# A WaveNet convolution block: the first loads in halves on two queues, fewer warm-up products, one extra tap moved, and the last gate on GpSimd

## The chip, the cores and the metric

The kernel runs on one core of a Trainium2 chip. A core has TensorE (PE in the profile, for matrix products, with PEld for the load of the fixed operand), VectorE (DVE), ScalarE (ACT), GpSimd (POOL), SyncE (SP, which issues transfers) and 16 DMA engines that all queues share. The metric is the device time of one execution in microseconds (us), and lower is better. Times are compared as medians of several runs.

## The reference

`x` is a batch of 2 sequences of 16000 time steps with 256 channels, in bfloat16. A causal convolution with three taps and dilation 2 gives 512 channels. The first 256 go through tanh, the others through a sigmoid, their product is projected by a 256x256 matrix.

```python
dil, K = 2, 3
pad = (K - 1) * dil                      # 4 rows of zeros ahead
xp = jnp.pad(x, ((0, 0), (pad, 0), (0, 0)))
h = sum(einsum('btc,cd->btd', xp[:, pad - i*dil : pad - i*dil + T], w[i]) for i in range(K))
z = jnp.tanh(h[..., :D]) * sigmoid(h[..., D:])
out = z @ w_o
```

So tap `w[0]` meets the step itself, `w[1]` the step two back and `w[2]` the step four back.

## The kernel before, in words

**Groups and blocks.** Time is cut into groups. The first group is *plain*: 512 steps of sequence 0, done with the three taps as they stand. Fifteen *wide* groups of 2048 steps follow; they use a fast scheme in which sums and differences of `x` (tiles `q`, `qp`, `qm`, `qd`, made on VectorE and GpSimd) meet combined weights (`wmh`, `wph`, `wm`, `wt`, `wu`, `wd0`, `wd2`), so that fewer products are needed. Two small plain groups fill what is left: `extra` (512 steps, tiles `e_ps`, input `xte`) is mixed into the first wide blocks, and `end` (256 steps, input `xe`, tiles `th`, `sg`, `z`) is done at the end. Each group has four blocks of 128 output channels, in the order tanh, sigmoid, tanh, sigmoid (`O_ORDER`). The order of all instructions is written out by hand, and the order in the program is the order on each engine.

**The head.** `xn` (named `osb` in the profile) is the plain input with time on the partitions. SP's queue issues `xn`, then the tap `w[0]`, and then the transposing loads `xq` of the first wide group (L119), `xte` (L105) and `xq` of the second. ScalarE's queue issues taps `w[2]` and `w[1]` (`TAPS` is (2, 0, 1), the order in which the plain blocks use them) and then loads its activation table (L135). TensorE meanwhile does 14 products of a tile of zeros, 256 columns each (L140). Then `turn` transposes `xn` on TensorE in eight 128x128 pieces (L184), ScalarE and VectorE copy the results into `xt` (L186), and 40 products of the four plain blocks follow (L311, function `direct`). VectorE and ScalarE form the combined weights as the taps arrive (L421 to L426); two of them are made on TensorE by `weight_mm` (L172). The first wide blocks begin with `first` (L255), which reads `qp`.

**A wide block** in the steady loop runs on TensorE: `late(V, 0)` for the block before it (L247, weights `wt` and `wu`), `second` (weights `wph`, input `qm`), the projection of finished gates (L366), `first` of the next block, `third` (weights `wm`, input `qm`), and `late(V, 1)` (weights `wd2`, `wd0`). Between them stand `keep_second` on ScalarE (L281, tile `sv`), which `third` waits for, `split_bank` on VectorE (L287), which reads what `third` wrote and which `late(V, 0)` of the next iteration waits for, `other` on GpSimd (L284) and `rest` on VectorE (L291). Index `ND` (4) is the first wide block. `extra_block(i, taps)` does block `i` of the extra group for the taps given; its activation follows the last tap.

**The tail.** After the last wide block the four remaining projections of the group before (`left`, in two pairs), eight of the last group (`last_pieces`), and the end group are finished. `plain_ends` does the end group's convolution for tanh or sigmoid (L311) and its activation on ScalarE (L587); `gate(end, ...)` is its product on VectorE (L342), written so that four time phases interleave; its projection is one `out_mm` with its copy at L649 and its store at L650. `gate_phases` gates half of the last group (L593). `last_pieces` copies one projected piece on ScalarE and one on VectorE (both L615) and stores them (L624, or each on a queue of its own, L617). Tiles named `o_ps` have two buffers, so a projection that uses one waits until the copy two projections back is done.

Of the kernel before, what the change touches and what calls it, by code (L numbers as in the profile page):

```python
# [8 lines left out]
ACT = mybir.ActivationFunctionType  # L9
# [4 lines left out]
def kernel(  # L14
# [23 lines left out]
    nc = tc.nc  # L38
# [4 lines left out]
    P = 128  # L43
# [8 lines left out]
    TAPS = (2, 0, 1)  # L52
# [4 lines left out]
    for b in range(B):  # L57
        t, stop = (4 * 2 * P if b == 0 else 0), (T - 4 * RE if b == B - 1 else T)
        while t < stop:
            n = min(need, (stop - t) // 8)  # L60
# [8 lines left out]
    end = dict(wide=False, b=B - 1, r0=T // 4 - RE, R=RE, g="z")  # L69
# [18 lines left out]
    def new_y():  # L88
        return ps_y.tile([P, 2, BANK], f32, name="y")
# [38 lines left out]
    w_taps = [consts.tile([P, CT, D2], bf16, name=f"w{k}_sb") for k in range(K)]  # L128
    wo_sb = consts.tile([P, NT, D], bf16)
    xn = osb_pool.tile([P, 4, D], bf16, name="osb")  # L130
    w_in = [w[k].rearrange("(ct c) d -> c ct d", c=P) for k in range(K)]
    nc.sync.dma_start(out=xn[:], in_=x[0, 0:4 * P, :].rearrange("(r j) c -> r j c", j=4))
    for k in (TAPS[0], TAPS[2]):
        nc.scalar.dma_start(out=w_taps[k][:], in_=w_in[k])
    nc.scalar.preload_act_table(ACT.Sigmoid)  # L135
    nc.sync.dma_start(out=w_taps[TAPS[1]][:], in_=w_in[TAPS[1]])
    for n in range(14):
        if n < 6 and n % 2 == 0:
            wps = new_y()
        nc.tensor.matmul(  # L140
            wps[:, 1, (n % 2) * 256:(n % 2 + 1) * 256], lhsT=warm[:, :P], rhs=warm[:, :256],
            start=n % 2 == 0 and n < 6, stop=True, skip_group_check=True,
        )
# [149 lines left out]
    def direct(B, taps, out, new=True, h0=None):  # L293

        xt, R = B.G["x"], B.R
        if B.G is not end:
            xp, yp, xc, yc = views(B.G)
        for tap in taps:
            if B.G is end:
                parts = [(None, xt[:, 4 - 2 * tap:8 - 2 * tap])]  # L300
            elif tap == 1:
                parts = [(0, yp), (1, xc)]
            elif h0 is not None:
                parts = [(h0, (xp, yp)[h0])]
            else:
                lo = RH if tap == 0 else RH - 1
                parts = [(None, xt[:, :, :, lo:lo + R])]
            for h, mv in parts:
                to = out if h is None else out[:, 2 * h * R:2 * (h + 1) * R]
                for ct in range(CT):  # L310
                    nc.tensor.matmul(  # L311
                        to, lhsT=w_taps[tap][:, ct, B.osl], rhs=mv[:, :, ct, :],
                        start=new and tap == TAPS[0] and ct == 0 and not h, stop=tap == TAPS[-1] and ct == CT - 1,
                        skip_group_check=True,
                    )
# [9 lines left out]
    def activate(B, src):  # L325
        G = B.G
        act_tiles(G)
        o = B.o
        func = ACT.Tanh if o < NT else ACT.Sigmoid
        dst = G["th"][:, o] if o < NT else G["sg"][:, o - NT]  # L330
        if src == "sv":
            nc.scalar.activation(out=dst[:, 2:4, :], in_=B.sv[:], func=func, scale=0.25)  # L332
        elif src == "y":
            nc.scalar.activation(out=dst[:, 0:2, :], in_=B.y[:], func=func, scale=0.25)  # L334
        else:
            nc.scalar.activation(out=dst, in_=src.rearrange("p (j r) -> p j r", j=4), func=func, scale=1.0)

    def gate(G, dts, eng=nc.vector):
        z = G["z"][:, dts]
        if G is end:  # L340
            z = z.rearrange("p t r j -> p t j r")
        return eng.tensor_tensor(out=z, in0=G["th"][:, dts], in1=G["sg"][:, dts], op=ALU.mult)  # L342
# [60 lines left out]
    ND = 4  # L403
# [39 lines left out]
    def extra_block(i, taps):  # L443
        E = extras[i]
        if TAPS[0] in taps:
            E.y = ps_o.tile([P, BANK], f32, name="e_ps", tag="o_ps")
        direct(E, taps, E.y[:])
        if TAPS[-1] in taps:
            activate(E, E.y[:])
# [11 lines left out]
    def do(steps, k):  # L461
        ins = None
        for step in steps.pop(k, []):
            ins = step() or ins
        return ins
# [36 lines left out]
    for k in range(ND, NB):  # L502
        B, V = blocks[k], (blocks[k - 1] if k > ND else None)

        E = {ND: (0, TAPS[2:]), ND + 1: (1, TAPS[2:]), ND + 2: (2, TAPS), ND + 3: (3, TAPS)}.get(k)
        if k == ND + 1:
            extra_block(1, TAPS[:2])
        if V:
            late(V, 0)
        if k >= ND + 2:  # L510
            Y = blocks[k - 2]
            activate(Y, "y")
            note_gates(Y, k)
        last = do(small, k) or last

        big_late = k == ND + 1

        def big_and_quarter(last):
            last = do(big, k) or last
            if B.oi == 0 and k > ND:  # L520
                quarter(B.G, 3, last)
            elif B.oi and B.G["n"] + 1 < len(wides):
                quarter(wides[B.G["n"] + 1], B.oi - 1, last)
            return last

        if not big_late:
            last = big_and_quarter(last)
        second(B)
        keep_second(B)
        other(B, last)  # L530
        if V:
            rest(V)
        if E:
            extra_block(*E)
        if k == ND + 3:
            gates_of(extra, slice(0, 2))

        project(0 if k < ND + 3 else 1 if k < ND + 7 else 2)
        evict()
        N = blocks[k + 1] if ND < k < NB - 1 else None  # L540

        split_first = k in (ND + 2, ND + 3) or k >= ND + 7
        if N:
            first(N, 0)
            if not split_first:
                first(N, 1)
        third(B)
        split_bank(B)
        if big_late:
            last = big_and_quarter(last)  # L550
        if V:
            activate(V, "sv")
        if N:
            if split_first:
                first(N, 1)
            keep_first(N)
        if V:
            late(V, 1)
        todo += ready
        ready.clear()  # L560
        if B.oi == 0:
            if loaded_wide < len(wides):
                load_wide(loaded_wide)
                loaded_wide += 1
            elif "x" not in end:
                load_end()
# [14 lines left out]
    def plain_ends(func, i):  # L581

        for h in range(NT):
            B = ends[2 * h + i]
            direct(B, TAPS, ye[:, i, h * 4 * RE:(h + 1) * 4 * RE], h == 0)
        dst = end["sg" if i else "th"]
        nc.scalar.activation(  # L587
            out=dst[:].rearrange("p h j r -> p (h j r)"), in_=ye[:, i, :NT * 4 * RE], func=func, scale=1.0)
# [3 lines left out]
    def gate_phases(ps):  # L592
        nc.vector.tensor_tensor(out=G["z"][:, dt, ps], in0=G["th"][:, dt, ps], in1=G["sg"][:, dt, ps], op=ALU.mult)  # L593
# [11 lines left out]
    left = [todo[i:i + 2] for i in range(0, len(todo), 2)]  # L605
# [3 lines left out]
    def last_pieces(rb0, jps, where, queues=None):  # L609
        two_pieces([(G, rb0, jp) for jp in jps], where)  # L610
        osb = osb_pool.tile([P, 2, 2, D], bf16, name="osb")
        rows = out[b, t0 + 8 * rb0:t0 + 8 * (rb0 + P), :].rearrange("(p j) d -> p j d", j=8)
        at = [rows[:, 2 * jp:2 * jp + 2, :] for jp in jps]
        for i, (jp, copy) in enumerate(zip(jps, (nc.scalar.copy, nc.vector.tensor_copy))):
            copy(out=osb[:, i], in_=G["o", rb0, jp])  # L615
            if queues:
                queues[i].dma_start(out=at[i], in_=osb[:, i])  # L617
        if not queues:

            dims = [list(d) for d in at[0].ap]  # L620
            both = bass.AP(
                tensor=at[0].tensor, offset=at[0].offset,
                ap=[dims[0], [2 * (jps[1] - jps[0]) * D, 2], [1, 2 * D]])
            nc.sync.dma_start(out=both, in_=osb[:].rearrange("p i q d -> p i (q d)"))  # L624

    def left_pieces(ps, where, between=None):
        two_pieces(ps, where)
        if between:
            between()
        for i, piece in enumerate(ps):  # L630
            out_evict(*piece, i == 1)

# [5 lines left out]
    left_pieces(left[0], "o")  # L638
    last_pieces(0, (1, 2), "y")
    gate_phases(slice(0, 2))  # L640
    last_pieces(P, (1, 2), "o")
    plain_ends(ACT.Sigmoid, 1)
    left_pieces(left[1], "yy", lambda: gate(end, slice(0, 2)))
    last_pieces(0, (0, 3), "o")
    (piece,) = pieces(end)
    out_mm(*piece, y_bank(new_y(), 0))
# [2 lines left out]
    nc.scalar.copy(out=osb[:], in_=end["o", 0, None])  # L649
    nc.sync.dma_start(  # L650
        out=out[end["b"], te:te + 4 * RE, :].rearrange("(q p) d -> p q d", q=2), in_=osb[:])
    last_pieces(P, (0, 3), "o", (nc.scalar, nc.sync))


# [28 lines left out]
```

## Time and profile before

| | us |
|---|---|
| time, median of 3 runs | 265.46 (265.1 to 265.76) |
| the profiled execution's own time | 265.18 |
| its span, first to last instruction | 263.4 |
| TensorE busy | 257.0 (98%) |
| ScalarE busy | 246.5 (94%) |
| VectorE busy | 226.6 (86%) |
| GpSimd busy | 111.2 (42%) |

A row of the timeline gives the start and the duration in us, the engine, the line of the kernel, the operation, the tile written and the tiles read, the size and the count; rows of one kind that follow each other are merged. In square brackets stands how long the engine had been idle, and what ended that. A "q" behind an engine's name is its queue of transfers. Records of matrix products overlap, since they are pipelined: one of 256 columns lasts 0.27 us, but the next starts 0.11 us after it.

### The profile page before, as it was taken

The page shows a single profiled execution, that of the slowest core. Times are in us where ns is not written, and L with a number is a line of the kernel's source. Part 1 is how long each engine was busy: PE and PEld are TensorE (multiplying, and loading weights), DVE is VectorE, ACT ScalarE, POOL GpSimd, SP SyncE. Part 2 cuts the span into 40 slices and gives each one's busy share as a digit, 9 for nine tenths or more (in the row PEclk, how much of TensorE's full clock was granted, in tenths as well). Part 3 has the DMA queues.
Part 4 walks back from the last instruction along what each step waited for, and adds up shares of the span by engine and source line. Part 5 has one row for each costly group of instructions (what it writes and reads, how often), then busy time and mean ns, then how long its engine had stood idle before and what let it go on. Part 6 is the DMA issues. An engine that isn't in the chain of part 4 may idle for free.

```text
span 263.4 us, 4233 instructions
## 1 busy us (share of the span) xinstructions
PE 257.0 (98%) x1469; PEld 144.0 (55%) x1470; DVE 226.6 (86%) x262; ACT 246.5 (94%) x377; POOL 111.2 (42%) x128
## 2 busy tenths in 40 slices
PE   7999999999999999999999999999999999999993
PEld 6544544555555555555555555555555555555682
DVE  3779899898898998899889889889889988976574
ACT  3858899999999999999999999999999999999972
POOL 1025345535534544544553553454454354353200
PEclk9999999999999999999999999999999999999999
DMA  7997092472928339192762819357292834221235
GB/s 204 221 149 160 0 206 78 105 193 79 212 80 176 116 110 218 55 238 80 111 181 99 231 42 197 133 94 197 82 213 76 186 126 101 80 80 42 82 119 179
DMA packets 78789, 35.10 MB, mean 133 GB/s; under 512 B 69168, under 2 KB 70960, under 8 KB 78768
## 3 DMA queue, kind: packets, MB, share of 16 engines
q1 hardware_dynamic: 77808, 34.05, 51.8%
q10 hardware_dynamic: 960, 0.79, 1.1%
q8 instruction: 11, 0.18, 0.3%
q14 instruction: 10, 0.08, 0.1%
HBM read 1.18 MB, written 16.38 MB: 67 GB/s over the span
## 4 chain that ended last, share of the span: by engine, by line
PE 92%; DVE 5%; issue 1%; ACT 1%; DVEq 0%
PE y L247 56%; PE o_ps L366 19%; PE y L255 9%; PE y L311 3%; DVE sv L291 1%; PE e_ps L311 1%; PE y L140 1%; PE y L172 1%; DVE y L287 1%; PE y L366 1%; DVE qp L220 1%; DVE osb L615 1%; DVE q L214 0%; DVE zw L342 0%; DVE z L342 0%
## 5 line engine op out<-in xcount | busy, mean ns | idle before, releaser
L284 POOL TENSOR_TENSOR sv<-sv,st 128x512 f32<-128x512 f32 x60 | 76.4, 1273 | 25.1 <-ACT sv L281 24.7
L232 POOL TENSOR_TENSOR qd<-xq 128x256 bf16<-128x256 bf16 (+2 forms) x60 | 35.4, 592 | 110.7 <-DVE zw L342 54.0
L291 DVE TENSOR_TENSOR sv<-sv,y 128x1024 f32<-128x1024 f32 x60 | 72.7, 1212 | 3.8 <-PE y L247 3.7
L247 PE MATMUL y<-qd,wd_sb 128*128 128x512 bf16 x240 | 61.6, 379 | 0.4 <-DVE sv L291 0.3
L395 ACT CAST osb<-o_ps 128x512 bf16<-128x512 f32 x113 | 60.6, 591 | 0.2 <-PE o_ps L366 0.2
L366 PE MATMUL o_ps<-wo_sb,zw 128*128 128x256 bf16 x464 | 60.3, 273 | 0.1
L287 DVE SCALAR_TENSOR_TENSOR y<-st,y 128x512 f32<-128x512 f32 x60 | 41.8, 696 | 20.6 <-PE y L247 20.4
L366 PEld LDWEIGHTS <-zw 128*128 128x128 bf16 x480 | 47.0, 98 | 17.4 <-issue 0.2
L255 PE MATMUL y<-qp,wmh_sb 128*128 128x512 bf16 x120 | 44.3, 379 | 0.0
L247 PEld LDWEIGHTS <-wd_sb 128*128 128x128 bf16 x240 | 23.4, 98 | 29.1 <-issue 1.5
L281 ACT ACTIVATE sv<-y 128x512 f32<-128x512 f32 x60 | 35.8, 597 | 2.9 <-PE y L247 2.7
L214 DVE TENSOR_TENSOR q<-xq 128x2048 bf16<-128x2048 bf16 (+2 forms) x32 | 36.8, 1155 | 1.3 <-DMA xq<-in_x_dram 1.3
L277 ACT ACTIVATE st<-y 128x512 f32<-128x512 f32 x60 | 36.3, 607 | 0.0
L247 PE MATMUL y<-qm,wm_sb 128*128 128x512 bf16 x120 | 35.7, 379 | 0.2 <-ACT sv L281 0.2
L247 PE MATMUL y<-q,wu_sb 128*128 128x512 bf16 x120 | 35.7, 379 | 0.0
L247 PE MATMUL y<-q,wt_sb 128*128 128x512 bf16 x120 | 35.7, 379 | 0.0
L247 PE MATMUL y<-qm,wph_sb 128*128 128x512 bf16 x120 | 35.7, 379 | 0.0
L342 DVE TENSOR_TENSOR zw<-thw,sgw 128x2048 bf16<-128x2048 bf16 x29 | 35.3, 1218 | 0.0
L332 ACT ACTIVATE sgw<-sv 128x1024 bf16<-128x1024 f32 x30 | 32.3, 1078 | 0.9 <-DVE sv L291 0.9
L332 ACT ACTIVATE thw<-sv 128x1024 bf16<-128x1024 f32 x30 | 32.3, 1078 | 0.1
L334 ACT ACTIVATE sgw<-y 128x1024 bf16<-128x1024 f32 x30 | 31.3, 1043 | 0.1
L334 ACT ACTIVATE thw<-y 128x1024 bf16<-128x1024 f32 x30 | 31.3, 1044 | 0.0
(65 smaller groups left out, 173.9 us busy)
## 6 DMA issues: line engine op xcount, KB each, us to landing
out_dram<-osb SPq DMA_DIRECT2D x59, 256.0 KB, 2.1
w_sb<-in_w_dram ACTq DMA_DIRECT2D x2, 256.0 KB, 4.1
out_dram<-osb SPq DMA_DIRECT2D x2, 160.0 KB, 2.0
osb<-in_x_dram SPq DMA_DIRECT2D x1, 256.0 KB, 2.5
w_sb<-in_w_dram SPq DMA_DIRECT2D x1, 256.0 KB, 4.2
xq<-in_x_dram SPq DMA_TRANSPOSE x16, 7.0
out_dram<-osb SPq DMA_DIRECT2D x2, 96.0 KB, 2.2
wo_sb<-in_w_o_dram ACTq DMA_DIRECT2D x1, 128.0 KB, 6.5
```

What stands on the lines that cost most here:

```text
L214: ins = nc.vector.tensor_tensor(out=sums(G, "q")[:, h, :, :, :, sl].rearrange("p h q ct r -> p h (q ct) r"), in0=s, in1=a, op=ALU.subtract ...
L247: nc.tensor.matmul(B.y[:, bank, :], lhsT=wmat[:, ct, B.osl], rhs=mv[:, :, ct, :], start=False, stop=ct == CT - 1, skip_group_check=True,)
L255: nc.tensor.matmul(B.y[:, 0, :], lhsT=W["wmh"][:, ct, B.osl], rhs=B.G["qp"][:, :, ct, :], start=ct == 0, stop=ct == CT - 1, skip_group_che ...
L277: nc.scalar.mul(B.st[:], B.y[:, 0, :], 4.0)
L281: nc.scalar.mul(B.sv[:, 0], B.y[:, 0, :], 2.0)
L284: after(nc.gpsimd.tensor_tensor(out=B.sv[:, 1], in0=B.sv[:, 0], in1=B.st[:], op=ALU.subtract), behind)
L287: nc.vector.scalar_tensor_tensor(out=B.y[:, 1, :], in0=B.st[:], scalar=-0.5, in1=B.y[:, 0, :], op0=ALU.mult, op1=ALU.add)
L291: nc.vector.tensor_tensor(out=B.sv[:], in0=B.sv[:], in1=B.y[:], op=ALU.subtract)
L332: nc.scalar.activation(out=dst[:, 2:4, :], in_=B.sv[:], func=func, scale=0.25)
L334: nc.scalar.activation(out=dst[:, 0:2, :], in_=B.y[:], func=func, scale=0.25)
L366: nc.tensor.matmul(o_ps[:, q, :], lhsT=z_columns(G, rb0, jp, q, dt), rhs=wo_sb[:, dt, :], start=(dt == 0), stop=(dt == NT - 1),)
L395: copy(out=G["osb"][:, 2 * h:2 * h + 2, :], in_=o_ps)
```

## The change

The change has five parts.

1. `xn` is loaded in two halves of its partitions, one on SP's queue and one on ScalarE's. Tap `w[2]` follows in two halves of its channels, one on each queue; then `w[0]` on SP's queue and `w[1]` on ScalarE's. Each queue has three issues where it had two, ahead of SP's transposing loads and ScalarE's table load.
2. There are 10 warm-up products in place of 14.
3. The first tap (`w[2]`) of extra block 1 is computed one iteration earlier, behind the last tap of extra block 0 and ahead of `third` of the first wide block. The second tap stays where it was.
4. In the tail, the sigmoid products of the end group come ahead of the pair (1, 2) of the last group's second half, where they came behind it, and the gate of the end group goes from VectorE to GpSimd, straight behind its sigmoid.
5. The last two stores swap queues: the piece copied by ScalarE goes out on SP's queue, the one copied last by VectorE on ScalarE's.

```diff
-    nc.sync.dma_start(out=xn[:], in_=x[0, 0:4 * P, :].rearrange("(r j) c -> r j c", j=4))
-    for k in (TAPS[0], TAPS[2]):
-        nc.scalar.dma_start(out=w_taps[k][:], in_=w_in[k])
+    x_in = x[0, 0:4 * P, :].rearrange("(r j) c -> r j c", j=4)
+    for h, queue in enumerate((nc.sync, nc.scalar)):
+        rows = slice(h * P // 2, (h + 1) * P // 2)
+        queue.dma_start(out=xn[rows], in_=x_in[rows])
+    for ct, queue in enumerate((nc.sync, nc.scalar)):
+        queue.dma_start(out=w_taps[TAPS[0]][:, ct], in_=w_in[TAPS[0]][:, ct])
+    for k, queue in zip(TAPS[1:], (nc.sync, nc.scalar)):
+        queue.dma_start(out=w_taps[k][:], in_=w_in[k])
     nc.scalar.preload_act_table(ACT.Sigmoid)
-    nc.sync.dma_start(out=w_taps[TAPS[1]][:], in_=w_in[TAPS[1]])
-    for n in range(14):
+    for n in range(10):
...
         if k == ND + 1:
-            extra_block(1, TAPS[:2])
+            extra_block(1, TAPS[1:2])
...
         if E:
             extra_block(*E)
+        if k == ND:
+            extra_block(1, TAPS[:1])
...
-    def left_pieces(ps, where, between=None):
+    def left_pieces(ps, where):
         two_pieces(ps, where)
-        if between:
-            between()
         for i, piece in enumerate(ps):
             out_evict(*piece, i == 1)
...
     gate_phases(slice(0, 2))
+    plain_ends(ACT.Sigmoid, 1)
+    gate(end, slice(0, 2), nc.gpsimd)
     last_pieces(P, (1, 2), "o")
-    plain_ends(ACT.Sigmoid, 1)
-    left_pieces(left[1], "yy", lambda: gate(end, slice(0, 2)))
+    left_pieces(left[1], "yy")
     last_pieces(0, (0, 3), "o")
     (piece,) = pieces(end)
     out_mm(*piece, y_bank(new_y(), 0))
...
-    last_pieces(P, (0, 3), "o", (nc.scalar, nc.sync))
+    last_pieces(P, (0, 3), "o", (nc.sync, nc.scalar))
```

## The prediction

> **What bounds the kernel now.** I read the page first, for its shares and the chain that ended last. The second line below is the chain by engine.
>
> ```profile
> span 263.4 us, 4233 instructions
> ...
> PE 92%; DVE 5%; issue 1%; ACT 1%; DVEq 0%
> ```
>
> TensorE holds 92% of the chain. Between the head (the first 14 us) and the tail (the last 12) nothing is changed but one small move, so a gain has to come from starting TensorE's row of work earlier, or from ending it sooner. The profiled execution took 265.18 us for this span of 263.4, so 1.78 us lie around it; it ran 0.28 us below the median of 265.46. The sum is made against 265.18, and 0.28 is added at the end. I take 0.3%, or 0.8 us, as what a measurement can tell from no change.
>
> Next the chain in order of time, over the first 14 us (start, length, what):
>
> ```profile
> 1.19 3.17 PE y L140 x14
> ...
> 5.04 5.42 PE y L311 x40
> ...
> 10.72 2.32 PE y L172 x10
> 13.05 0.86 PE y L255 x4
> ```
>
> The chain goes through the warm-up products themselves: not the load of x but the 14 products decide when the transposes begin. Then the timeline of the head:
>
> ```profile
> 1.67 6.39 SPq L119 DMA_TRANSPOSE xq<-in_x_dram  x1
> 1.75 1.28 ACT L135 ACT_TABLE_LOAD   x1 [1.75 <-issue]
> ...
> 4.15 0.45 PE L184 MATMUL tp<-ident,osb 128*128 128x128 bf16 x4
> ...
> 5.48 1.22 DVE L421 TENSOR_TENSOR ws_sb<-w_sb 128x1024 f32<-128x1024 bf16 x1
> ...
> 9.61 0.60 ACT L336 ACTIVATE th<-y 128x512 bf16<-128x512 f32 x1 [0.43 <-PE y L311]
> 10.43 1.23 DVE L214 TENSOR_TENSOR q<-xq 128x2048 bf16<-128x2048 bf16 x1 [1.33 <-DMA xq<-in_x_dram]
> 11.69 0.69 DVE L220 TENSOR_TENSOR qp<-q 128x1024 bf16<-128x1024 bf16 x1
> 12.88 1.03 PE L255 MATMUL y<-qp,wmh_sb 128*128 128x512 bf16 x4
> 13.44 1.28 DVE L223 TENSOR_TENSOR qm<-q 128x1024 bf16<-128x1024 bf16 x2
> 14.64 0.59 PE L247 MATMUL y<-qm,wph_sb 128*128 128x512 bf16 x2
> ```
>
> VectorE waits 1.33 us for the first wide load and ends `qp` at 12.38, 0.50 us ahead of the product that reads it. Two chains run beside each other: TensorE's, which is late, and that of the wide load, which has half a microsecond to spare.
>
> **Part 1 and 2: loads and warm-up products.** The 14 products took 1.19 to 4.15, which is 0.211 us each; x had been issued at 0.74 and took 2.5 us (timeline, then the issues with KB and us to landing):
>
> ```profile
> 0.74 0.41 SPq L132 DMA_DIRECT2D osb<-in_x_dram  x1
> 0.74 0.98 ACTq L134 DMA_DIRECT2D w_sb<-in_w_dram  x2
> ```
>
> ```profile
> osb<-in_x_dram SPq DMA_DIRECT2D x1, 256.0 KB, 2.5
> w_sb<-in_w_dram ACTq DMA_DIRECT2D x2, 256.0 KB, 4.1
> ```
>
> So x is there at 3.24, and 0.9 us of warm-up products lie behind that. Ten end at 1.19 + 2.11 = 3.30, just as x lands. I count nothing for an earlier x: its 256 KB go through the same DMA engines either way, and after 3.30 the transposes no longer wait for products; a landing 0.2 us later would cost those 0.2 us. The taps on ScalarE's queue took 4.1 us (the median of two), and in the new order tap 2 still has only x ahead of it; it is wanted at about 4.4.
>
> What of the 0.85 us (3.30 against 4.15) reaches L311? Before, the first transpose to the first of the 40 products took 5.04 − 4.15 = 0.89. The warm-up products ran at half the rate of later ones: 0.211 us for 256 columns, where the tail's L366 rows below do eight in 0.87, 0.109 each. Four transposes ahead of the second copy, at the slow rate, cost some 0.2 us more. So L311 begins at 3.30 + 0.89 + 0.2 = 4.39, 0.65 earlier. ScalarE, with a third issue of about 0.49, ends its table load near 3.03 + 0.49 = 3.5, ahead of its copy at some 3.75. The 40 products need `w[0]` after 16 of them (1.7 us, so at 6.1), `w[1]` later still; before, VectorE used `w[0]` (with `w[2]`, L421) at 5.48. That covers it by 0.6 us.
>
> TensorE would reach L255 at 12.88 − 0.65 = 12.23, but `qp` ends at 12.38. With 0.06 to pass it on, L255 starts at 12.44: **0.44 us earlier**, if the wide load lands as before. That load lies behind the same 512 KB on SP's queue and the same 1 MB in all, so I keep its landing. But SP issues one transfer more ahead of it (0.49 for one on ScalarE's row), so the bound is from 0 later to 0.49 later, and the gain from 0.65 (should the load come earlier, too) down to 0. I take 0.44: SP had ended that issue at 8.06, and VectorE got the data 2.4 us later, so the transfers in the queue, not the start of the issue, seem to set the landing. ScalarE is free in time: its first activation had waited 0.43 for TensorE. Downstream, `second` at 14.64 moves to 14.20 and finds `qm`'s first half, ended at about 14.1.
>
> **Part 3: the extra tap.** The timeline of the first wide block:
>
> ```profile
> 15.07 0.60 PE L311 MATMUL e_ps<-xte,w_sb 128*128 128x256 bf16 x4
> 15.27 0.60 ACT L281 ACTIVATE sv<-y 128x512 f32<-128x512 f32 x1 [0.19 <-PE y L247]
> ...
> 15.92 0.59 PE L247 MATMUL y<-qm,wm_sb 128*128 128x512 bf16 x2 [0.24 <-ACT sv L281]
> ...
> 16.35 1.03 PE L311 MATMUL e_ps<-xte,w_sb 128*128 128x512 bf16 x4
> 16.63 0.69 DVE L287 SCALAR_TENSOR_TENSOR y<-st,y 128x512 f32<-128x512 f32 x1 [1.30 <-PE y L247]
> ...
> 17.38 0.59 PE L247 MATMUL y<-q,wt_sb 128*128 128x512 bf16 x2
> ```
>
> `third` (15.92) waits for ScalarE's `sv` (ends 15.87); `late` (17.38) waits for VectorE's L287 (ends 17.32). Four products of 512 columns from 16.35 took 0.86 of issue. Two of them (0.43) fit ahead of `third`: 15.07 + 0.43 + 0.43 = 15.93. But their old place does not close: `late` still waits for L287, which waits for `third`. The hole moves from ahead of `third` to behind it. **Nothing**, from 0.05 lost (two products just too long) to 0.1 gained; its cover is that hole, and without it the two products would cost 0.43 wherever they stand.
>
> **Part 4 and 5: the tail.** Its timeline, then the two forms of GpSimd's work, with count, busy us, mean ns and idle time:
>
> ```profile
> 254.27 1.47 PE L311 MATMUL y<-xe,w_sb 128*128 128x256 bf16 x12
> 255.58 1.04 PE L366 MATMUL y<-wo_sb,zw 128*128 128x256 bf16 x8
> ...
> 256.40 1.30 DVE L342 TENSOR_TENSOR z<-th,sg 128x512 bf16<-128x512 bf16 x1 [0.31 <-ACT sg L587]
> 256.45 1.04 PE L366 MATMUL o_ps<-wo_sb,zw 128*128 128x256 bf16 x8
> 257.13 0.59 ACT L615 CAST osb<-o_ps 128x512 bf16<-128x512 f32 x1 [0.28 <-PE o_ps L366]
> 257.50 0.72 DVE L395 CAST osb<-y 128x512 bf16<-128x512 f32 x1
> ...
> 258.14 0.67 DVE L615 CAST osb<-o_ps 128x512 bf16<-128x512 f32 x1
> 259.50 0.69 DVE L615 CAST osb<-o_ps 128x512 bf16<-128x512 f32 x1 [0.69 <-PE o_ps L366]
> 260.22 0.34 SPq L617 DMA_DIRECT2D out_dram<-osb  x1
> ```
>
> ```profile
> L284 POOL TENSOR_TENSOR sv<-sv,st 128x512 f32<-128x512 f32 x60 | 76.4, 1273 | 25.1 <-ACT sv L281 24.7 <-POOL qd L232 0.3
> L232 POOL TENSOR_TENSOR qd<-xq 128x256 bf16<-128x256 bf16 x52 | 32.3, 622 | 103.0 <-DVE zw L342 50.4 <-DVE q L214 28.9 <-PE y L247 20.6
> ```
>
> VectorE's gate of 1.30 us stands ahead of two copies, L395 and L615. The second frees the `o_ps` buffer for the very last four products, whose result VectorE copies at 259.50; the store goes out at 260.22, and the span ends 3.18 later. Without the gate, L395 starts when its products are done (256.62) and ends at 257.3; L615 starts when its own are done, at 256.45 + 1.04 = 257.49, in place of 258.14. That is 0.65 earlier. The chain behind it (four products, copy, store) has no other late partner: the first of the last pair needs the buffer that ScalarE frees at 257.72, and the end group's four products now stand at 257.33 to 257.76 in TensorE's order. **0.63 us**, taking 0.02 off for the hand-over.
>
> The sigmoid products take 1.31 us of issue (255.58 − 254.27) and move ahead of eight projections of 0.87. They start at 254.27 − 0.87 = 253.40 and end near 254.87; the activation (0.60) ends near 255.5. GpSimd's gate has 512 elements per partition. Its nearest rows give 1.24 (two times 0.622) to 1.27; the interleaved output, for which VectorE took 1.30 where 1024 elements in order take 0.69 (L220), could double it. So z is there between 256.8 and 258.1; I take 256.8, by GpSimd's own rows. TensorE asks for it at 257.33: it may take 1.8 us before it costs anything. What waits behind GpSimd's gate is nothing; it has no later work.
>
> The pair (1, 2) is now projected at 254.71 and copied by 256.5, a time at which its buffers are not yet wanted (256.89 for the second). The swapped queues cost or gain at most the difference of landing of the stores, 0.3 lost to 0.2 gained; both issues last about 0.35, and I take zero.
>
> **Sum.** 265.18 − 0.44 − 0 − 0.63 = 264.11; plus 0.28 gives **264.4 us** against 265.46, a gain of 1.07. With the bounds of its own terms (head 0.25 to 0.65, tail 0.35 to 0.8) this case runs from 263.9 to 264.9.
>
> **The rivals.** *The wide load comes later.* If SP's additional issue delays the load by its 0.49, `qp` ends at 12.87, L255 starts at 12.93 and the head's gain is gone; the tail's stays: 265.46 − 0.63 = 264.83. For it: VectorE waits 1.33 us on this load, so any delay is passed on at once. Against it: the transfers ahead of it carry the same bytes.
>
> *GpSimd's gate is the new wait.* At double the price (2.55 us) z comes at 258.05, the end group's products end at 258.55 and the last four start near 259.0, against 258.87 before. The tail's gain is lost: about 265.1. For it: the output's pattern. Against it: 0.5 us of slack.
>
> *TensorE runs slow for longer, and the kernel is slower.* The page grants the full clock everywhere, but the spacing of the products says half rate until about 4.15, after 2.96 us of unbroken products. With ten, 2.11 us of products are followed by transposes and a short gap. If the rate then rises only after another 2.96 us of products from 4.39 on, half of that, 1.48 us, is lost. L311 ends 1.48 − 0.65 = 0.83 later than before, and the tail returns 0.63: 265.46 + 0.83 − 0.63 = 265.66. It decides from where the loss passes the two gains, 0.65 + 0.63 = 1.28, which is 2.56 us of slow products; were all 40 slow (5.2 us at the full rate, so 5.2 more), it would be 269.4. For it: before, only one stretch of the trace shows what lifts the rate. Against it: the transposes are TensorE work and fill the same time.
>
> [...]
>
> **How the numbers follow.** The forecast gets 0.62, the late load 0.12, the slow gate 0.08, the slow rate 0.18. The border at 0.8 us is 264.66: of the forecast's 0.62 some 0.54 lie below it; of the load's 0.12, 0.05; of the gate's 0.08, 0.02; that gives 0.61 faster. Slower by over 0.8 us is 266.26: 0.11 of the slow rate and 0.01 each of the other two, 0.13. The rest, 0.26, is no change. The range has the forecast's ends with 0.2 more on the low side for the spread of the runs before, and takes in the late load and the slow gate with their spread: 263.7 to 265.5. Most of the slow rate, some 0.16, is left out.
>
> **What would show it.** Right: L140 x10 ending near 3.5, L311 starting near 4.4, the q row (L214) still near 10.4, L255 near 12.4; the hole of 0.6 us behind the first `third`; no L342 row of VectorE for `z`, a GpSimd row of about 1.3 us ending before 257 on the old scale, and the last store some 1.07 us earlier in the span. Wrong: products of L311 that follow each other by 0.21 us; L214's wait for `xq` ending at 10.8 or later; TensorE waiting for GpSimd at the end group's products; or a steady stretch that does not keep the head start.

## The result, and the profile after

| | before | changed |
|---|---|---|
| median of 9 runs, us | 265.46 (265.06 to 265.96) | 267.02 (265.87 to 267.76) |
| the profiled execution's own time, us | 265.18 | 267.07 |
| its span, us | 263.4 | 265.3 |

The changed kernel is slower: the ratio of its times to those of before is 1.0051, with a 95% interval of 1.0029 to 1.0072. Its times also spread more than those of before, three near 266.0 and six between 267.0 and 267.8. In the experiments, one slow run each of `e1_old_loads` (339.88), `e5_x_split` (703.83) and `e10_gate_dve` (457.14) counts in the median that is given and not in the ratio, so that the fast runs of `e5_x_split` have a median of 268.59 where its row says 268.93.

The chain of work that ended last, in order of time, over the head of the changed kernel (start, length, what; L315 are the 40 plain products, L176 `weight_mm`, L259 `first`):

```profile
0.73 0.58 SPq L135
1.31 0.06 issue
1.37 4.45 DMA w_sb<-in_w_dram
5.82 0.05 issue
5.87 6.97 PE y L315 x40
...
13.11 2.32 PE y L176 x10
15.43 0.86 PE y L259 x4
```

The warm-up products are gone from the chain, as forecast, but a transfer has taken their place: a half of tap 2, issued at 1.37, holds TensorE until 5.82. And the 40 products behind it take 6.97 us, where they took 5.42. The timeline shows the rest of the head:

```profile
0.73 0.58 SPq L135 DMA_DIRECT2D osb<-in_x_dram  x1
0.74 0.56 ACTq L135 DMA_DIRECT2D osb<-in_x_dram  x1
...
1.37 0.83 SPq L137 DMA_DIRECT2D w_sb<-in_w_dram  x1
...
3.96 0.58 PE L188 MATMUL tp<-ident,osb 128*128 128x128 bf16 x4 [0.46 <-DMA osb<-in_x_dram]
...
5.87 6.97 PE L315 MATMUL y<-xt,w_sb 128*128 128x256 bf16 x40 [0.90 <-DMA w_sb<-in_w_dram]
...
11.41 1.23 DVE L218 TENSOR_TENSOR q<-xq 128x2048 bf16<-128x2048 bf16 x1 [0.39 <-DMA xq<-in_x_dram]
...
15.27 1.03 PE L259 MATMUL y<-qp,wmh_sb 128*128 128x512 bf16 x4
```

Each issue of half of x lasts 0.58 or 0.56 where the whole took 0.41, and SP's issue behind it 0.83. x comes 0.46 us after TensorE is ready for it, tap 2 another 0.90 late, the wide load is used at 11.41 in place of 10.43, and the first wide block begins at 15.27 in place of 12.88. One stretch of the windows view shows the DMA engines (the last three columns are the granted clock, the share of the 16 engines and the rate in GB/s), first of the kernel before, then of the changed one:

```profile
3.80:4.80 1.00, 1.00 (x11) 0.72 (x9) 0.17 (x1) 0.28 (x2) 0.00 (x0) 1.00 0.92 317
```

```profile
3.80:4.80 1.00, 0.84 (x8) 0.78 (x8) 0.22 (x1) 0.38 (x2) 0.00 (x0) 1.00 0.54 137
```

With all three taps still to come, the engines move 137 GB/s where they moved 317. The product rate, by the same source line in a stretch of the head (duration in ns as min/median/max, then first and last start), changed kernel first, then the kernel before:

```profile
L315 PE MATMUL y<-xt,w_sb x6: 413/417/417, 7.8 to 8.8; 128*128 128x256 bf16 x6
```

```profile
L311 PE MATMUL y<-xt,w_sb x12: 272/273/273, 5.3 to 6.5; 128*128 128x256 bf16 x12
```

417 ns is about the length that the warm-up products have too (median 421 before), and the next starts 0.21 us after it, where it was 0.11. So the products ran at half rate up to about 9.0, while the clock column says 1.00. The tail, last:

```profile
258.00 1.35 POOL L346 TENSOR_TENSOR z<-th,sg 128x512 bf16<-128x512 bf16 x1 [7.92 <-ACT sg L593]
...
259.07 0.69 DVE L399 CAST osb<-y 128x512 bf16<-128x512 f32 x1 [0.18 <-PE y L370]
...
259.75 0.60 PE L370 MATMUL y<-wo_sb,z 128*128 128x256 bf16 x4
...
261.33 0.69 DVE L621 CAST osb<-o_ps 128x512 bf16<-128x512 f32 x1 [0.69 <-PE o_ps L370]
...
262.05 0.37 ACTq L623 DMA_DIRECT2D out_dram<-osb  x1
```

GpSimd's gate takes 1.35 us and ends at 259.35, before TensorE asks. From the last wide products to the span's end the kernel before took 263.4 − 250.78 = 12.62, the changed one 265.3 − 253.21 = 12.09. The account closes: head +2.39 (0.83 for the later start of the 40 products, 1.55 for their rate), the stretch between +0.04 (237.90 against 237.94), tail −0.53, in all +1.90 against +1.89 of the two profiled times.

### The profile page after: what moved, and what is told of

Its sections match the earlier page's. It is cut to its first block, busy times and chain, and to the rows that moved or that the text cites. A ratio compares the mean times of both kernels' runs of the same rounds, so it can differ in the third digit from the quotient of the medians.

```text
span 265.3 us, 4229 instructions
## 1 busy us (share of the span) xinstructions
PE 257.9 (97%) x1465; PEld 144.3 (54%) x1466; DVE 225.7 (85%) x261; ACT 246.7 (93%) x377; POOL 112.7 (42%) x129
## 4 chain that ended last, share of the span: by engine, by line
PE 91%; DVE 5%; DMA 2%; issue 1%; ACT 0%; SPq 0%; DVEq 0%
PE y L251 56%; PE o_ps L370 19%; PE y L259 9%; PE y L315 4%; DMA w_sb<-in_w_dram 2%; DVE sv L295 1%; PE e_ps L315 1%; DVE y L291 1%; PE y L176 1%; PE y L370 1%; DVE qp L224 1%; DVE q L218 0%; DVE zw L346 0%; DVE osb L621 0%; DVE z L346 0%
## 5 line engine op out<-in xcount | busy, mean ns | idle before, releaser
L259 PE MATMUL y<-qp,wmh_sb 128*128 128x512 bf16 x120 | 44.3, 379 | 0.0
```

What stands on the lines that cost most here:

```text
L259: nc.tensor.matmul(B.y[:, 0, :], lhsT=W["wmh"][:, ct, B.osl], rhs=B.G["qp"][:, :, ct, :], start=ct == 0, stop=ct == CT - 1, skip_group_che ...
```

## The experiments

All ratios are to the kernel before, measured on the same chip in the same hours. The last three rows come from another chip than those from `e1_old_loads` to `e10_gate_dve`, so between them it is the ratios that compare.

| kernel | head loads | warm-up | extra tap | tail | median us | ratio, 95% interval |
|---|---|---|---|---|---|---|
| changed | changed | 10 | moved | new | 267.02 | 1.0051 (1.0029 to 1.0072) |
| e1_old_loads | old | 10 | moved | new | 264.54 | 0.9966 (0.9953 to 0.9979) |
| e2_14_warm | changed | 14 | moved | new | 265.63 | 1.0011 (0.9996 to 1.0025) |
| e3_tail_only | old | 14 | old | new | 264.76 | 0.9974 (0.9964 to 0.9985) |
| e7_10_warm | old | 10 | old | old | 265.45 | 0.9998 (0.9986 to 1.0010) |
| e5_x_split | x in halves of partitions | 14 | old | old | 268.93 | 1.0099 (1.0066 to 1.0131) |
| e6_w_split | tap 2 in halves | 14 | old | old | 265.56 | 1.0002 (0.9993 to 1.0012) |
| e9_tail_extra | old | 14 | moved | new | 264.95 | 0.9976 (0.9965 to 0.9987) |
| e10_gate_dve | old | 14 | old | new, gate on VectorE | 265.15 | 0.9988 (0.9977 to 0.9998) |
| e11_x_split_rows | x in halves of rows | 14 | old | old | 265.55 | 1.0009 (0.9999 to 1.0019) |
| e12_x_split_one_queue | x in halves of partitions, SP alone | 14 | old | old | 268.83 | 1.0125 (1.0101 to 1.0149) |
| e13_changed_x_rows | changed, x in halves of rows | 10 | moved | new | 265.07 | 0.9979 (0.9967 to 0.9991) |

**First round: loads, warm-up products, tail.** The changed kernel with the old loads:

```diff
-    for h, queue in enumerate((nc.sync, nc.scalar)):
-        queue.dma_start(out=xn[rows], in_=x_in[rows])
...
+    nc.sync.dma_start(out=xn[:], in_=x[0, 0:4 * P, :].rearrange("(r j) c -> r j c", j=4))
+    for k in (TAPS[0], TAPS[2]):
+        nc.scalar.dma_start(out=w_taps[k][:], in_=w_in[k])
...
+    nc.sync.dma_start(out=w_taps[TAPS[1]][:], in_=w_in[TAPS[1]])
```

> The changed kernel with the loads of the kernel before put back (x whole on SP's queue, taps 2 and 1 on ScalarE's, tap 0 on SP's); ten warm-up products, the moved extra tap and the new tail stay. In the changed kernel's profile tap 2 was ready only at 5.82 us and the 40 products (L315) took 6.97 us in place of 5.42. Theory A (the split loads are the cause of both: they make tap 2 late, and the pause that this gives TensorE keeps it at half rate): L315 starts near 4.4 and takes about 5.4, and the kernel comes out near 264.4, 1.0 faster than before. Theory B (ten warm-up products alone are too few for the full rate): L315 starts near 4.4 but takes 6.7 to 7.0, and the time is about 265.7, the same as before within 0.3.

The loads turn 267.02 into 264.54, as theory A says. Its timeline:

```profile
3.72 0.61 PE L184 MATMUL tp<-ident,osb 128*128 128x128 bf16 x4 [0.21 <-DMA osb<-in_x_dram]
...
4.66 5.83 PE L311 MATMUL y<-xt,w_sb 128*128 128x256 bf16 x40
...
12.92 1.03 PE L255 MATMUL y<-qp,wmh_sb 128*128 128x512 bf16 x4
```

The 40 products begin at 4.66 and take 5.83, between the two theories' numbers, and the first wide block begins no earlier than before (12.88). So the gain of 0.34% does not come from the head.

The changed kernel with 14 warm-up products:

```diff
-    for n in range(10):
+    for n in range(14):
```

> The changed kernel with 14 warm-up products in place of ten, all else as changed. Theory A (the split loads make tap 2 late): L315 starts near 5.8 whatever the number of warm-up products; if the long pause ahead of it is what holds the rate down, the 40 products still take 6 to 7 us and the time stays near 267; Theory B (the number of warm-up products holds the rate down): 40 products in 5.4 us, the start still at 5.8, so about 1.5 less than the changed kernel, 265.5.

```profile
5.69 5.32 PE L315 MATMUL y<-xt,w_sb 128*128 128x256 bf16 x39 [0.30 <-DMA w_sb<-in_w_dram]
...
13.44 1.03 PE L259 MATMUL y<-qp,wmh_sb 128*128 128x512 bf16 x4
```

The start stays late (5.69, theory A), the rate is full (5.32, theory B), and the time is theory B's, 265.63. So the loss has two parts that can be taken apart: the late tap alone costs 0.56 in the head (13.44 against 12.88), about what the tail wins; the half rate, which 14 products avoid with these loads, costs the rest.

Ten warm-up products alone, in the kernel before:

```diff
-    for n in range(14):
+    for n in range(10):
```

> The kernel before with ten warm-up products in place of 14 and nothing else. Theory A (ten are enough where tap 2 comes in time): L311 starts near 4.4, takes 5.4, and 0.4 to 0.65 is won: about 265.0. Theory B (ten are too few): L311 starts near 4.4 and takes up to 7.0: 265.46 + 0.8 to 0.95 = about 266.3.

Neither number: the ratio is 0.9998.

```profile
3.78 0.61 PE L184 MATMUL tp<-ident,osb 128*128 128x128 bf16 x4 [0.28 <-DMA osb<-in_x_dram]
...
4.73 5.65 PE L311 MATMUL y<-xt,w_sb 128*128 128x256 bf16 x40
...
12.80 1.03 PE L255 MATMUL y<-qp,wmh_sb 128*128 128x512 bf16 x4
```

x comes at 3.73, not at 3.24 (the issues view has 3.0 us to landing here, 2.5 to 3.1 over the runs with old loads). The 40 products start 0.31 earlier and lose 0.23 of that to a rate that rises later (near 5.3, against about 4.2 in the profile of before).

The new tail alone, in the kernel before:

```diff
...
+    plain_ends(ACT.Sigmoid, 1)
+    gate(end, slice(0, 2), nc.gpsimd)
     last_pieces(P, (1, 2), "o")
-    plain_ends(ACT.Sigmoid, 1)
-    left_pieces(left[1], "yy", lambda: gate(end, slice(0, 2)))
+    left_pieces(left[1], "yy")
...
-    last_pieces(P, (0, 3), "o", (nc.scalar, nc.sync))
+    last_pieces(P, (0, 3), "o", (nc.sync, nc.scalar))
```

> The kernel before with the tail of the changed one alone (sigmoid products of the end group earlier, its gate on GpSimd, the last stores' queues swapped). From the start of the last wide products to the end of the span the kernel before took 263.4 - 250.78 = 12.62 us and the changed one 265.3 - 253.21 = 12.09. If the tail is worth this by itself: 265.46 - 0.53 = 264.9. If the two profiles differed there only by chance, or the tail gained only because the head came late: 265.46 within 0.2.

It is worth 0.26% (0.15 to 0.36), or 0.7 us, and 12.62 becomes 262.9 − 251.01 = 11.89 in its profile.

**Second round: which load, and which part of the tail.** x in halves of its partitions, tap 2 whole:

```diff
-    nc.sync.dma_start(out=xn[:], in_=x[0, 0:4 * P, :].rearrange("(r j) c -> r j c", j=4))
+    for h, queue in enumerate((nc.sync, nc.scalar)):
+        rows = slice(h * P // 2, (h + 1) * P // 2)
+        queue.dma_start(out=xn[rows], in_=x_in[rows])
...
```

> The kernel before with only x loaded in two halves on the two queues (tap 2 whole on ScalarE's queue behind its half, then tap 1; tap 0 on SP's; 14 warm-up products; old tail). In the changed kernel with 14 warm-up products the loads alone made L315 start at 5.69 in place of 5.04 and cost about 0.55 us. Theory A1 (the halves of tap 2 are what comes late): this kernel is the same as before, 265.5, with L311 at 5.0 to 5.1. Theory A2 (the halves of x delay all that follows): tap 2 ready after 5.4, about 266.0.

Theory A2, and worse: 268.93. TensorE waits for tap 2 until 6.42 and again, for tap 1, until 11.85:

```profile
6.42 3.67 PE L314 MATMUL y<-xt,w_sb 128*128 128x256 bf16 x24 [1.44 <-DMA w_sb<-in_w_dram]
11.85 1.94 PE L314 MATMUL y<-xt,w_sb 128*128 128x256 bf16 x16 [1.75 <-DMA w_sb<-in_w_dram]
```

The queues' rows suggest why it is worse than the changed kernel's own loads with 14 products (265.63): behind its two long issues, tap 1 is issued only after SP's wide load.

```profile
1.36 0.86 ACTq L136 DMA_DIRECT2D w_sb<-in_w_dram  x1
...
2.00 9.68 SPq L119 DMA_TRANSPOSE xq<-in_x_dram  x1
2.25 0.49 ACTq L137 DMA_DIRECT2D w_sb<-in_w_dram  x1
```

In the changed kernel and in `e2_14_warm` the last tap is issued ahead of the wide load. That this order makes the difference is read from these rows; no run tests it alone. The rate is another matter. Right behind the pause of 1.44 us it is full (first products of L314):

```profile
L314 PE MATMUL y<-xt,w_sb x10: 272/273/285, 6.4 to 7.4; 128*128 128x256 bf16 x10
```

Tap 2 in halves, x whole:

```diff
+    for ct, queue in enumerate((nc.sync, nc.scalar)):
+        queue.dma_start(out=w_taps[TAPS[0]][:, ct], in_=w_in[TAPS[0]][:, ct])
...
```

> The kernel before with only tap 2 loaded in two halves (x whole on SP's queue, then the first half of tap 2 and tap 0; the other half and tap 1 on ScalarE's queue; 14 warm-up products; old tail). Theory A1 (the halves of tap 2 come late, the one behind x on SP's queue above all): L311 waits until about 5.5, time about 266.0. Theory A2 (the halves of x are at fault): the same as before, 265.5.

The same as before (1.0002), so the halves of tap 2 are free. The new tail with the moved tap, on top of `e3_tail_only`:

```diff
-            extra_block(1, TAPS[:2])
+            extra_block(1, TAPS[1:2])
...
+        if k == ND:
+            extra_block(1, TAPS[:1])
```

> The kernel before with the new tail and the moved extra tap, old loads, 14 warm-up products. If the moved tap is worth nothing: the same as the new tail alone, 264.76 within 0.2. If the moved tap is the 0.2 by which the changed kernel with old loads (264.54) was below the new tail alone: 264.5.

0.9976 against 0.9974 of the tail alone: the moved tap is worth nothing that can be measured. From the first to the second `first` the chain takes 19.39 − 13.13 = 6.26 with it and 19.27 − 13.05 = 6.22 in the kernel before. The new tail with the gate on VectorE:

```diff
-    gate(end, slice(0, 2), nc.gpsimd)
+    gate(end, slice(0, 2))
```

> The kernel before with the new tail, but the end group's gate left on VectorE at its new, earlier place. If taking 1.30 us from VectorE's row is what wins: the gate now runs from about 255.5 to 256.8 and pushes the three copies behind it, so the last copy starts no more than 0.2 earlier than before (259.5) and the time is 265.3 to 265.5. If the earlier sigmoid is what wins: 264.8, as with GpSimd.

```profile
255.69 1.30 DVE L342 TENSOR_TENSOR z<-th,sg 128x512 bf16<-128x512 bf16 x1
256.79 0.72 DVE L615 CAST osb<-o_ps 128x512 bf16<-128x512 f32 x1
257.43 0.67 DVE L395 CAST osb<-y 128x512 bf16<-128x512 f32 x1
258.19 0.69 DVE L615 CAST osb<-o_ps 128x512 bf16<-128x512 f32 x1
```

The gate does push the three copies, and 265.15 lies below the first number and above the second: the tail is worth 0.12% so and 0.26% with GpSimd, with intervals (0.02 to 0.23, 0.15 to 0.36) that overlap. GpSimd seems to bring about half. The swapped stores are in both kernels and were not run alone, so the other half can be theirs or that of the earlier sigmoid.

**Third round: why halves of x are slow.** Halves by rows, on both queues, against `e5_x_split`:

```diff
-        queue.dma_start(out=xn[rows], in_=x_in[rows])
+        queue.dma_start(out=xn[:, 2 * h:2 * h + 2], in_=x_in[:, 2 * h:2 * h + 2])
```

> The kernel before with x in two halves on the two queues, but cut by the rows that each partition holds (128 partitions, two of the four rows each), where the changed kernel cuts by partitions (64 partitions, all four rows). With halves by partitions, the same kernel took 268.93, its x issues lasted 0.58 us in place of 0.41 and tap 2 came at 6.4. Theory P (a transfer to half of the partitions is what is slow): here the issues last 0.41, L311 starts near 5.0 and the time is 265.5. Theory Q (x on both queues at once, or tap 2 behind it on ScalarE's queue, is what is slow, whatever the cut): L311 after 5.8, about 267 to 269.

Halves by partitions, both on SP's queue, against `e5_x_split`:

```diff
-    for h, queue in enumerate((nc.sync, nc.scalar)):
+    for h, queue in enumerate((nc.sync, nc.sync)):
         rows = slice(h * P // 2, (h + 1) * P // 2)
```

> The kernel before with x in two halves of its partitions, both on SP's queue (ScalarE's queue as before: taps 2 and 1). Theory P (the half of the partitions is slow by itself): issues of 0.58 again and a late tap 0 or wide load, 266.5 to 269. Theory Q (the two queues are what matters): issues of 0.41, and 265.5 to 265.8, since only SP's row is one issue longer.

The two answer the question. By rows an issue lasts 0.40 or 0.41 again and the time is that of before within 0.2%; by partitions on one queue alone the time is 268.83. The timelines, rows first:

```profile
0.74 0.41 SPq L134 DMA_DIRECT2D osb<-in_x_dram  x1
...
5.12 5.54 PE L313 MATMUL y<-xt,w_sb 128*128 128x256 bf16 x40
```

```profile
0.73 1.21 SPq L135 DMA_DIRECT2D osb<-in_x_dram  x2
...
6.33 0.58 PE L187 MATMUL tp<-ident,osb 128*128 128x128 bf16 x4 [1.98 <-DMA osb<-in_x_dram]
...
7.25 6.62 PE L314 MATMUL y<-xt,w_sb 128*128 128x256 bf16 x40
```

Theory P, as to the time: the cut by partitions is what is slow, not the two queues. What comes late is not the same, though: on one queue it is x itself (TensorE waits for it until 6.33, and not for tap 0 or the wide load, as theory P had it), on two queues the taps. So the nearly equal times need not have one cause. The changed kernel with that one line in its row form:

```diff
-        queue.dma_start(out=xn[rows], in_=x_in[rows])
+        queue.dma_start(out=xn[:, 2 * h:2 * h + 2], in_=x_in[:, 2 * h:2 * h + 2])
```

> The changed kernel with its x halves cut by rows instead of partitions, all else as changed (ten warm-up products too). Theory P: tap 2 is ready by about 4.6, L315 starts there and takes 5.4 to 5.8, and the time is 264.5 or a little less, as with the old loads. Theory Q: as changed, about 267.

It is 0.21% faster than before (0.09 to 0.33), so the cut of x alone decides between slower and faster. In its profile (264.41, the fastest of its 12 runs) the 40 products go from 4.66, for 5.52, as expected; the first wide block starts at 12.60, 0.28 before that of the kernel before. The median of 265.07 is above the 264.5 expected, and not told apart from `e1_old_loads` or `e3_tail_only` by their intervals. `e1_old_loads` has the lowest median of all, 264.54, faster than both kernels.

The changed kernel once more, without any edit, for a profile of its lower group:

> The changed kernel once more, for a second profile. Its nine times fell into 265.9 to 266.1 (three) and 267.0 to 267.8 (six). If the moment at which TensorE's rate rises sets the group: a profile of the lower group has the 40 products (L315) in about 5.4 to 5.8 us from the same start near 5.8, one of the upper group again about 7.0; if the loads set it, the start differs and the 40 products take the same.

It took 266.19 in one run, the lower group's time or close to it. Both halves of the expectation were too simple:

```profile
4.22 0.61 PE L188 MATMUL tp<-ident,osb 128*128 128x128 bf16 x4 [0.72 <-DMA osb<-in_x_dram]
...
5.17 6.72 PE L315 MATMUL y<-xt,w_sb 128*128 128x256 bf16 x40
```

The start is 0.70 earlier than in the other profile: TensorE waits 0.72 for x, and the profile shows no wait for tap 2 behind it. The products are slow there, too, until about 7.8. So the moment at which the loads land differs from run to run (x ended TensorE's wait at 4.22 here, at 3.96 in the other profile), half rate is in both profiles, and a late tap 2 is not needed for it. The first wide block begins at 14.40, 0.87 before that of the other profile, which is all but 0.01 of the 0.88 us between the two times.

## Why the prediction was wrong

**The loads (the step that failed).** The prediction counted nothing for x in halves, since "its 256 KB go through the same DMA engines either way", and took it that tap 2, with "only x ahead of it", would be there at about 4.4. It came at 5.82 in the profile. Its own row gave no ground for 4.4: 4.1 us to landing, the median of two taps, is 4.84 from the old issue at 0.74, and tap 2 was now to be issued later. No row of the kernel before showed a load to 64 partitions, so that cost should have been bounded from both sides; it was instead set by the bytes, and the bound of 0.2 us for a late x was never carried to tap 2. The loads by themselves cost 0.56 us in the head (`e2_14_warm`); `e11_x_split_rows` and `e12_x_split_one_queue` put it on the cut by partitions. That the halves of tap 2 cost nothing held (`e6_w_split`, 1.0002), and so did the third issue on each queue (`e13_changed_x_rows`: issues of 0.41 to 0.46, the first wide block at 12.60). Against the sum of 264.11, the first wide block came 2.83 us after its 12.44, the tail won 0.10 less and the stretch between took 0.04 more: 267.08, where the profiled execution took 267.07.

Halves by rows, on the same queues and with the same bytes, cost nothing here (`e11_x_split_rows`, 1.0009), while halves by partitions cost about 1% (1.0099 in `e5_x_split`, 1.0125 in `e12_x_split_one_queue`).

**The warm-up products.** The prediction took x at 3.24 from one landing of 2.5 us; with ten products x held TensorE until 3.73 (`e7_10_warm`). Of the 0.65 at L311, 0.31 came, the later rise of the rate took 0.23, and 0.08 reached L255. The bound that was set there, `qp` at 12.38, was not what decided: TensorE was the later of the two.

**The slow rate.** This rival was the right mechanism with the wrong trigger. It was given 0.18 and 265.66, with ten products and a short gap as its cause. Ten products with a short pause did not bring it: in `e1_old_loads`, `e7_10_warm` and `e13_changed_x_rows` x held TensorE for 0.20 to 0.28 us and the rate is full by about 5.6. It came where x was later: with pauses of 0.46 for x and 0.90 for tap 2 in the changed kernel's first profile, where it cost 1.55 us, near the 1.48 worked out; with 0.72 for x alone in its second (6.72 − 5.42 = 1.30); and with 1.98 behind 14 products (`e12_x_split_one_queue`: 40 products in 6.62). Where the rate had risen before the pause, it stayed: in `e2_14_warm` the weight load of the product ahead of it, at 5.1, lasts 95 ns (146 at the slow rate), and the products behind the pause of 0.30 last 273; `e5_x_split` stood still for 1.44 and went on at full rate. So what goes with the slow rate, in these profiles, is a pause of 0.46 us or more before the rate has risen. That is read across kernels that differ in more than the pause; no run makes a pause by itself, and where the border between 0.28 and 0.46 lies was not measured. The prediction treated the late load and the slow rate as separate cases; they came together, and so the time passed not only the range up to 265.5 but the rival's own 265.66.

**The tail.** The 0.63 were right: 0.53 in the changed kernel's profile, 0.73 in the profile of `e3_tail_only`, 0.7 in its median. GpSimd's gate took 1.35 (1.27 forecast) and nobody waited for it. The working gave all of it to the gate's leaving VectorE; `e10_gate_dve` suggests that the earlier sigmoid or the swapped stores have a share of their own. If so, that its size came out right is in part luck.

**The extra tap.** Nothing, as forecast: 0.04 us longer in the chain, none in the median.

## What to carry to other kernels

A transfer's cost is not only its bytes (the same halves of x: 1.0009 by rows, 1.0099 by partitions): before a load is cut in two, look for a row with the same cut, and if there is none, give it a bound of its own and ask what waits behind it. Causes of one stage can come together: a late load made a pause, and behind such a pause TensorE stayed at half rate, which cost more than the load (1.55 us against 0.83). Warm-up products that only seem to delay the first use of a load can also be the cover that lets the rate rise when that load is late (with the same loads, 39 of the 40 products in 5.32 us behind 14 of them, all 40 in 6.97 behind ten).

## What the runs showed of the hardware

- A load of 64 partitions by 2 KB was issued in 0.56 to 0.58 us, one of 128 partitions by 1 KB (the same bytes) or by 2 KB in 0.40 or 0.41. The issue behind it was longer too (0.56 to 0.86, where it took 0.41 to 0.46 behind halves by rows), and in the changed kernel the DMA engines fell to 137 GB/s from 3.80 to 4.80 us, with work waiting (317 before). The trace also has, for each transfer, the sixteen moments at which its parts landed: those of the half of tap 2 that held TensorE came from 4.22 to 5.82 in the changed kernel, eight by 4.50 and eight from 5.28 on, those of the other half from 3.90 to 4.32, and those of the whole tap 2 in the kernel before from 3.66 to 4.02. So only some of the parts were late. Why, no run here shows.
- The product rate rose at different moments in kernels that are the same up to there: about 4.2 us in the profile of before, between 5.2 and 5.6 in that of `e3_tail_only`, both with 14 warm-up products. What decides the moment, and what part the transposes have in it, no run here shows: in `e7_10_warm` the rate rose near 5.3 with transposes between two rows of products.
- The granted clock column stayed at 1.00 while products took 417 ns in place of 273 (changed kernel, 7.8 to 8.8 us), so a slow rate has to be read from the products' own durations.
